# Two-layer grouped-query attention: transposing the probabilities of four batch steps per session, with Q projections in row tiles between them

## The chip, the core and the metric

The kernel runs on one NeuronCore of a Trainium2 chip. The metric is the device time of one execution in microseconds, as the median of a few runs. TensorE is called PE here (PEld for its weight loads), VectorE DVE, ScalarE ACT, GpSimd POOL, and SP is the queue that issues every DMA.

## The reference

Two independent problems, A and B, of the same shape; their results stand side by side in the output.

```python
B, Sq, D = 16, 80, 576
Hq, Hkv, Sk, Dh = 32, 16, 512, 128           # bf16 inputs
q = (x @ wq).reshape(B, Sq, Hq, Dh).transpose(0, 2, 1, 3)
k = jnp.repeat(k_cache, 2, axis=1)           # k_cache, v_cache: (B, Hkv, Sk, Dh)
v = jnp.repeat(v_cache, 2, axis=1)
p = softmax(einsum("bhqd,bhkd->bhqk", q, k) * Dh ** -0.5)
o = einsum("bhqk,bhkd->bhqd", p, v)
out = o.transpose(0, 2, 1, 3).reshape(B, Sq, Hq * Dh) @ wo
# concatenate([out_A, out_B], axis=-1)
```

## The kernel before

**Units.** One batch of one "octet" (four K/V heads, so eight query heads of 80 rows each) is a unit, called a batch step here; there are 128 of them, U = 0 to 127. The 640 query rows of a unit are cut into five blocks of 128: four "mains" (k = 1 to 4, one K/V head each) and one "remainder" (k = 0, 32 rows of each of the four heads).

**What PE does.** For every eight batches and one octet, eight Q projection steps (each two heads by four batches) are computed from `xT` and `wq_sb`: D = 576 is contracted as four full chunks of 128 rows (L565) and a tail of 64 rows, for which the two heads stand in the two halves of the array's rows (L578, `tile_position=(64 * h, 0)`). Scores of a main are one full matmul of 512 columns (L692); those of a remainder are four matmuls of 32 output columns side by side (L679, `tile_position=(0, 32 * g4)`). After the softmax the probabilities P are transposed on PE (L749) in halves of 64 rows, two at a time, against a 64-wide identity. Attention times V is L797, the output projection L843. So PE works in three shapes of the array: full (L565, L692, L797, L843), row tiles (L578, L749) and column tiles (L679). The text calls a stretch in one shape a visit, and a change from one shape to the next a switch.

**What the others do.** DVE takes each block's row maximum out of PSUM (L701), ACT the exponential with its sum (L705), DVE the reciprocal (L711), POOL the normalisation (L714). Copies out of PSUM (Q: L590/L591, transposed P: L766/L767 and, for remainders, L775/L776, attention output: L811, output projection: L855, L872) are shared between DVE and ACT. PSUM has eight banks of 512 fp32 columns.

**A transposition session.** Two units are transposed together: 80 matmuls into five banks, the remainders of both in the fifth. P lives in 12 slots for mains and 4 for remainders (`NPA`, `NPR`), its transpose in two (`NPT`). Scores of two units are made as a group (`GR = 2`), both remainders first. The attention output `oT` is kept for all sixteen batches of an octet pair; the output projection goes over five row blocks for one half of the 576 columns and then for the other (`n % NRT, n // NRT`).

**The order.** Nothing is scheduled at run time. Each operation belongs to a stream (for example `T`: transposes, `PV`, `S`: scores, `K`: loads of K), and the string `ORDER` lists one letter per operation: it fixes the order on every engine, the PSUM bank of each result (digits), and by an apostrophe whether ACT instead of DVE makes a copy. `finalize` then adds the semaphores. A load is also tied to the PE operation that stands ahead of it in the table, so it is not issued earlier than that:

```python
if op.eng == "pe":
    last_pe = op
elif op.paced and last_pe is not None:      # names that begin with "ld"
    deps[id(last_pe)] = last_pe
```

K comes in loads of 1 MB for two units (a transposing DMA, L645, in three slots), V in loads of 0.5 MB for one (L649, six slots).

Of the kernel before, what the change touches and what calls it, by code (L numbers as in the profile page):

```python
# [12 lines left out]
GR = 2  # L13
# [3 lines left out]
NPA = 12  # L17
NPR = 4
NPT = 2
NS = 32  # L20
# [26 lines left out]
NSS = 6  # L47
# [19 lines left out]
wDCCCCC'B'Httcc7cj6j4d3Ad5wBtgl7102wKNGtl6'F'E'H'Gk45Fj7mj1xNwj0b6utwwtbj3j2c7acxwNt'yw'Atc1cj4c6mj0cd7wBANwCC
DCCCDCCj3c1cttud6BCtgl2451'HwKNG'Fl0DCCj6t'Ej7b2j3bwwNGw'Ftt'ytj5c1j6cc0ms7QwNwttd4j2cj5d3CCc6ANwYwc'BtCCDCc1'
ActCQgl7026'K'H'Gl5Fk34'B'F'EGk07xaj1wuxtNxxuuj6mb5c3bj2uwyNwcd4d0mj7gwt'Atj6c5wNHtt'Kcj3b1j4j7wBbc6j2tNwwtCCC
DCCDCCyj3ctCwl0415'Atl7mwFN'Gj6c2tcj0wd4d3g'F'Gtmaj5wNBEwNj2'Htamj7c6j1cc4d0cwtAwNwKtDCCCCCDCCc6d5cc2ct'BACgl6  # L70
374tBK'H'Gl1Fk25Fmj0'E'Gxb3j4mc7cj6j1bwuxwNt'Autj2c7cc0wtwyNCj4j5cj3d6twNwwtwBNtDCDCCCCCCb1j4twAbc5acd0tt'y'Bg
l4327'K'Hl5G'Fk60'Ek14m'FGxxc2j7b3uxuNwNDCCCCj6ubctwxAc1j0c'ytuw'Bc5cj2d6c7j3tNwAwCCDcj4d1d5ttwNBad0tCggCl3274
'K'HNHG'F'Kl1mE'F'Gk56Uj2j3b0c4mj7cbCDCxwtc1cj2wtuwxABwj3'yutwj4j0d1b5j6Nwtttc2NwwCDCtcaj3j7bmtNAwwCCCCd0c2cmd
6'yt'Btd5Umggl7432K'H'Hl0j6GEwNNb1CCCCj3j4w'K'F'GtwFtc5cbj2c7aj0j6ct'A'ywwNwBtc4d1j3cd5j2td7c0cRwNwBt'AttDCDCC
Cd4ggl6203H'H'KKl1F'Gk54'Ek67'F'Gxxuc0cc1cj3b2j5uxxwBwNNuutt'ACCc4j6Rcmc1bwAj3j7cj4b5j0wBNw'yttwNwCDCCCDCCd1j3
bad6tttwt'yd2d7ggl5340'K'KHHNl6'G'Fk27j1'G'FExxj3uc4cc5j6j0cuANwwwc2mmcj4m'Bc7tcUaUb5t'Btd1j7wNwAtd3wDCCCCCj6t
wtj2mbd4wNtd0tNyDCCCggl2567'HKKN'Hl3'G'FCCCk14'F'GEj0j5xuxj6c2cc3j7cwAwwu'Btttb1j2bc4cj3d6mamj0wwNAttwNwtj4d7D
CCCCCDwd5c2ctd3tggyBHN'Kl4201l6'Gj7KHEw'Fj5j2j3ac0'F'Gcc4cwwNBwtt'Ac6j1cd7j4c0cb5t'At'BwNj2d3j6bCDCCCtwwNwtd0C
CDCCt'ytd2ggl5641H'K'HKl3F'Gk02'Ek76x'Guxc5mj1cb4c0Nwu'At'Fcj2bj1c5CCDxBNwywutmcj4maj3mc0b2cNwwxB'Attutj5d1j7b
j4d6Qd0wwwNCCCCDCCttNytd3ggl4725K'HKl1Fk36Ej4'G'F'H'Gj7xxNCCCDCj2c0mucc1cj5c3Awwu'Btwtwcb0j6bj4tNwAwtd2aQj7c3c  # L80
j1d5mCCtwNwtCDCtd6td4gNByNHgl1037'K'HKFl2'Gk56'Ej4'G'Fxj0CCCuxwwc1cc7j2cj3'Atutc5mcb1wwAaj4j6bc0j5tBwNwtttwyNj
2mcd7d4DCCDCCwNBtd1Cd3tggl6520'Hl7NKF'K'G'H'Gj3Cwj4b6j0tEwwbj2j1c3d5c'Fttwj7c4j0ct'ywNAwNCCCCDt'BtQc3cj1d2wwaQ
c4d6mmgcd7CCCDtt'AKHBgl0351'H'Kl4F'G'F'Ek62Gk70xb4c3j1cc5xuuxxwcj2j6bBwN'Autuj7j3mc5cc1j0ctzwwNwwNCDCCDCCCt'A'
Btb4j5tNwbd7j2ad3td6twzNtd1ggl0425'H'HCCCCKNKl7k16Exx'F'GOj3j0c2'G'FcuwAwumOj5c4j7cc1c'Bc2tcmb6j4wt'BtwANwj3d0
aj1d2j5mbtwtNwwtCCCCDCDNztd7Cd4tggl5163'K'Hl2'FNKHGk47'ECCDCj1'Gxj0j5'Fj6xc3ucwc2uOcc4Xctb7j1wAwAw'BtttwNbj3c0
j2cj4d5wtwzwNttmaOd1d7td2CCCDCCBggl4603'Hl5'H'KKNE'G'FCd7j2j1wwc0cc6cj4'F'GBwN'Attc3cc6cj5mj0j2b1Nwwwt'A'Bttj6
d3CCCDCCDwNtCCj5abd0twtd2zggmOl4156'K'KHHl7'Gk32k10'FxxE'Guu'FNxNxb4bc3cj6c2wzCCCDCucj7w'Auj1c5OXcj3c0mw'Btt'A
j2cmb6j7mwBNwttj0mabj3d4CtwNwzwd1tCCDtCgl7652Ht'Kl0k41'Gj6xNwb3'F'E'Gtj5d2Fwutd7j6c0cj4bc5xNwut'AwzNj1cd3d0XOj
6wwCCCCDCCtt'Bj4gmg'K'Htj1c5cOwNHwCDc7d2ttcad6j4NKA'BgCCCUl1035wKNG'Hl7k62Et'G'F'Fj4b0q3j7j1abc5xwx$wu'#tutNDC
DCCCcc3j4d6cwwAzBttc7cj5j1d0wwNtCCtROmc3cd4d2BANggl5371K'H'K'FHl6Gj4j2d5'FEwGwc6cj3mj7b0'AtwwNtc1cj4CCDCCtc2wc  # L90
amUtc6j3cANwt'Bj7CDj2bd4wNwzCCd1ttt'BCd3ggl2076'KH'KHl4G'Fk51G'Ek23'Fxmc6cOc0cj7j4xub5xNwwu'B'Attuj0bj7c1j6acw
xzNwu'AtwNtOc4mcj2Xb5j3j0d1CCCCDCwBwtttd7j4d6bNwwNztCCCDDCCtd3ggl4520HKNF'Kl1'H'Gk37Gj5'E'Fxj4XRmUc6Xcc1d2cuj0
c3xwwAut'Bcd7j6wtc5j1gj4ctwNAwwCDCj0b3t'KtBNwHttUj6d7mbmad4j5NwzCCCCtgl3120wNGF'K'Hl6tk47DCCCCj1d5'F'Ex'Gj6Oxu
wj2c3cc0acd4uwA'Btwc7j0d3ctNwAd1tgtgNHc6j2'KHw'KDCCCcj7'Bd3wCtl0645tGl1j2d7j6FwwN'F'E'Gj0twgc4cd5c1j2tt'ANKwcc
6cj0c7q4mmOcNBHwt'Aj3j1$w'#t'BtwNb6d2j7btwCCDCCCCDCtCgl1340'KzHl6'FOk27Fk15ax'G'E'Gxuxuj3mb6c4cbj7j2c0NxwAwuut
# [12 lines left out]
2cj0j5c7cb3uu'AwwNxbj2tb1j0tu'BCCyNwwttj3j5mmj6c4cj2d7wwNwwNtt'ADCCCCCDCbc0cd3Ud4Ut'y'Btd6ggl2051KKHNN'Hl3a'GC
CCCDk64E'Fj0xj7c5'F'Gxucc2j3j1cuAwj6b5ww'Btttwc2j4d0mcd7tRj3wNwNwAbj1tDCCCCtc6cd2w'ytd5tggBNKl4631'H'KNHl7'Fk2
0'Ej5GxxDC'G'Fuj4mac3cmj6c1j7cuwwAb2c0cj3'BtwtwtANwj5d1ttwCbc0j4cj7d3wNwyttBd6td5aCCCCDCgCgml2047'KNHKl3'Gj5HE  # L110
w'Fj1'G'Fj0j6c4cwNAc7tcaOc3cc5j2t'BANwwwcj4mb7'BtttDCCCCCwNtj5d1d0CCCDwd3mj2btwytd6ggl5427H'K'KHl1G'Fk06'Ek45G
x'Fxc7cc1cu'Auc2cmc3cj0BNxwCj1'A'ButxwNb6bj3wuttj7j0b4j1j2bawwyNtj6d7twwNtCCCDCCDtd0wyNd5CCCtd1ggl2643H'K'Hl0'
Gk57KENxx'FCCCDj6j1mQ'G'Fuc4j2cj3c0cuAww'Btwb5c4j0ctj6twANwwttmmabj7d1c4j2cd3mtCDwNwBNytd0CCCd6tggl2547'H'HKKN
l1'G'Fk60ECCj5'F'Gxj3Qc4cj2c1cj7xuwwAuab6j0c4ttj5bcc3wwNBwwtt'Attj2j1d7cd4d5NwwNBytCDCCCDCd0tCgg'KHl1326'Kl4'F
j0j7GHww'E'Fttb3j4bj2c1j0wGNwwNt'yCCCDCCCj5ad6cc4j3cmtwwN'Attc7j2cd0wBAttd5c1cd4CDCBggl1372HK'K'Hl6G'Fk54k10'E
'F'Gxc7cc6j3j2cxuAuj7mj5wNNxxwb4t'Bmbj6b3mmwywututtj2bwwzNc0cOj7Qaj4c1md5cttwNAwCDCCCCDCCd6d3d2CgttBHNgl0147'K
'Hl6NKG'Fk25CCCCD'Ej1xj3'F'Gwuc0Qcc6j4cj7xwBtb2j1j6mautwwAttbj5c3cwNwNwttj0d4c7cmd1d6CCDCtd5gwABztgl3072'KCl1N
HKGH'Fk54'Ej3'G'FxNwj0c7cOj6c2cj1uAwttc5cb7j0wxNwwAbt'Buttj6j3c2d5j1acd0wwwNttd4CCDCDCCCCCd6tggBzN'K'H'Kl2713C
Cl0HGF'Ej4d6j5'G'Fc1cc7cj3wNwAwttc0j4cj2'B'AtNwwj5c7d1Ocmmd0tCDCCj4t'BNwwtb3j2mtbwDCCCtd4azggl2357O'K'HKl1G'Fk
64Ek32'F'G'Hxc5cj7c0cc1u'A'Bcxxwxuuutc6cj0mb5BANj6j1j3bwwNzwtDCCj4b0ambj5ttNwtNwwtd7j2d3twztmd6d4CCCCCDCggl105  # L120
2'HKNH'Kl3'GCOk67j0'F'F'Gj4ExxNwwuutb1c5cj6c3cj2j7btwwAwNt'Btj4mc0cc5j3j6cd2wCDCttd7AwwNtCDCCCCd4td0zNBggl6513
# [16 lines left out]

class _Op:
    __slots__ = ("eng", "key", "seq", "emit", "reads", "writes", "dsem", "stream", "alloc", "alt",  # L140
                 "deps", "signals", "sidx", "waits", "clock", "name", "hard", "parts", "paced")


class _Sched:
# [33 lines left out]
    def arrange(self):  # L178
# [778 lines left out]
```

## Time and profile before

| | before |
|---|---|
| median of 3 runs (lowest, highest) | 713.65 us (713.46, 714.14) |
| span of the profiled execution | 711.6 us, 26075 instructions, granted clock 1.000 |
| profiled execution's own time | the runs' 713.46 to 714.14: 1.9 to 2.5 us lie around the span |
| PE busy | 702.5 us (99%) |
| ACT, DVE, POOL busy | 645.5, 613.3, 431.9 us |
| DMA | 160.72 MB, mean 226 GB/s |

Busy times count an instruction from its start to its end. Instructions of PE overlap each other, so how long a group of matmuls holds PE is read from the start of the group to the start of the next one, not from its busy time.

### The profile page before, as it was taken

How to read it: one execution, taken by the hardware profiler on the slowest of the kernel's cores; microseconds unless marked ns; L12 is line 12 of the kernel's file. 1: busy time of each engine (PE TensorE's matmuls, PEld its weight loads, DVE VectorE, ACT ScalarE, POOL GpSimd, SP SyncE). 2: the span in 40 equal slices, each digit the busy share in tenths (PEclk: the TensorE clock that was granted, in tenths of full speed). 3: DMA queues.
4: the chain of work that ended last, by engine and by line, in shares of the span. 5: the costliest groups of instructions: out<-in, count | busy, mean ns of one | idle time of the engine just before them, and what ended most of it. 6: DMA issues, size and time to landing. Idle time of an engine off the chain costs nothing.

```text
span 711.6 us, 26075 instructions
## 1 busy us (share of the span) xinstructions
PE 702.5 (99%) x10820; PEld 512.5 (72%) x10820; DVE 613.3 (86%) x1339; ACT 645.5 (91%) x1772; POOL 431.9 (61%) x650
## 2 busy tenths in 40 slices
PE   8999999999999999999999999999999999999998
PEld 4567677777777777777767777777777777777767
DVE  2999898889798888899989888889888989889894
ACT  2999999999999999989999899999999989999893
POOL 0567666656565566656656576565756666477572
DMA  8999999989899998999989999999799989888762
GB/s 210 252 256 260 261 245 239 253 230 255 182 250 230 246 223 217 222 254 253 227 233 242 226 261 177 270 214 218 215 237 242 241 214 253 220 210 188 171 157 82
DMA packets 374166, 160.72 MB, mean 226 GB/s; under 512 B 278560, under 2 KB 370976, under 8 KB 374048
## 3 DMA queue, kind: packets, MB, share of 16 engines
q1 hardware_dynamic: 374048, 159.05, 96.4%
q8 instruction: 86, 1.41, 0.8%
q14 instruction: 32, 0.26, 0.1%
HBM read 87.65 MB, written 2.95 MB: 127 GB/s over the span
## 4 chain that ended last, share of the span: by engine, by line
PE 96%; ACT 1%; DMA 1%; DVE 1%; issue 0%; SPq 0%
PE ps L843 22%; PE ps L797 20%; PE ps L565 19%; PE ps L692 16%; PE ps L749 11%; PE ps L679 4%; PE ps L578 4%; DMA wq_sb<-in_A_wq_dram 1%; ACT p_sb L705 1%; DVE negmax L701 1%; ACT pT L766 0%; ACT oT L811 0%; PE ps L421 0%; SPq L400 0%; DVE qT L591 0%
## 5 line engine op out<-in xcount | busy, mean ns | idle before, releaser
L714 POOL TENSOR_SCALAR p_sb<-p_sb,rinv 128x512 bf16<-128x512 bf16 x640 | 430.1, 692 | 261.2 <-DVE rinv L711 260.8
L705 ACT ACTIVATE p_sb<-ps,negmax 128x512 bf16<-128x512 f32 x640 | 439.3, 717 | 15.8 <-DVE negmax L701 13.3
L701 DVE TENSOR_REDUCE negmax<-ps 128x1 f32<-128x512 f32 x640 | 409.8, 677 | 17.5 <-PE ps L692 9.5
L797 PE MATMUL ps<-pT,v_sb 128*128 128x160 bf16 x2048 | 186.0, 233 | 0.9 <-ACT p_sb L705 0.5
L797 PEld LDWEIGHTS ps<-pT,v_sb 128*128 128x128 bf16 x2048 | 154.9, 98 | 38.8 <-ACT pT L775 3.0
L843 PE MATMUL ps<-wo_sb,oT 128*128 128x288 bf16 x1280 | 180.9, 286 | 0.7 <-issue 0.7
L692 PE MATMUL ps<-kT,qT 128*128 128x512 bf16 x512 | 170.4, 380 | 1.2 <-issue 0.9
L565 PE MATMUL ps<-xT,wq_sb 128*128 128x320 bf16 x1024 | 165.1, 299 | 1.6 <-DMA wq_sb<-in_A_wq_dram 1.2
L843 PEld LDWEIGHTS ps<-wo_sb,oT 128*128 128x128 bf16 x1280 | 123.2, 98 | 45.7 <-DVE pT L767 1.8
L705 ACT ACTIVATION_READ_ACCUMULATOR p_sb<-ps,negmax 128x1 f32 x640 | 149.2, 233 | 0.0
L565 PEld LDWEIGHTS ps<-xT,wq_sb 128*128 128x128 bf16 x1024 | 97.1, 98 | 43.9 <-issue 1.7
L766 ACT COPY pT<-ps 128x512 f32<-128x512 f32 x181 | 100.5, 606 | 6.7 <-PE ps L749 4.8
L591 DVE TENSOR_SCALAR qT<-ps 128x320 bf16<-128x320 f32 x119 | 54.6, 483 | 39.8 <-PE ps L578 39.6
L749 PEld LDWEIGHTS ps<-ident,p_sb 64*128 64x128 bf16 x5120 | 82.6, 95 | 7.8 <-ACT oT L811 1.1
L749 PE MATMUL ps<-ident,p_sb 64*128 64x64 bf16 x5120 | 85.8, 190 | 0.5 <-DVE qT L591 0.4
L590 ACT ACTIVATE qT<-ps 128x320 bf16<-128x320 f32 x137 | 55.3, 446 | 21.8 <-PE ps L578 21.4
L811 DVE CAST oT<-ps 128x320 bf16<-128x320 f32 x143 | 67.6, 478 | 5.4 <-PE ps L797 4.9
L692 PEld LDWEIGHTS ps<-kT,qT 128*128 128x128 bf16 x512 | 45.6, 97 | 27.2 <-ACT pT L766 6.6
L767 DVE COPY pT<-ps 128x1024 bf16<-128x1024 bf16 x75 | 50.0, 685 | 9.8 <-PE ps L749 9.5
L811 ACT CAST oT<-ps 128x320 bf16<-128x320 f32 x113 | 49.3, 450 | 3.9 <-PE ps L797 3.8
L711 DVE RECIPROCAL rinv<-rowsum 128x3 f32<-128x3 f32 (+1 forms) x256 | 39.8, 159 | 3.6 <-ACT p_sb L705 3.3
L679 PE MATMUL ps<-kT,qT 128*32 128x512 bf16 x512 | 36.8, 383 | 0.0
(33 smaller groups left out, 149.8 us busy)
## 6 DMA issues: line engine op xcount, KB each, us to landing
v_sb<-in_A_v_cache_dram SPq DMA_DIRECT2D x64, 512.0 KB, 5.4
v_sb<-in_B_v_cache_dram SPq DMA_DIRECT2D x64, 512.0 KB, 4.9
wo_sb<-in_A_wo_dram SPq DMA_DIRECT2D x8, 576.0 KB, 5.8
wo_sb<-in_B_wo_dram SPq DMA_DIRECT2D x8, 576.0 KB, 5.9
wq_sb<-in_B_wq_dram SPq DMA_DIRECT2D x4, 1024.0 KB, 6.0
out_dram<-osb SPq DMA_DIRECT2D x40, 72.0 KB, 3.8
wq_sb<-in_A_wq_dram SPq DMA_DIRECT2D x8, 256.0 KB, 4.6
wq_sb<-in_A_wq_dram SPq DMA_DIRECT2D x2, 1024.0 KB, 6.0
```

What stands on the lines that cost most here:

```text
L565: last = e.matmul(ps[:, vbq[h].phys, QO:QO + 320], lhsT=wq_sb[:, wsl, ck, hi * 128:(hi + 1) * 128], rhs=xT[:, half, ck, n0:n0 + 320], star ...
L590: return e.activation(dst, src, AF.Identity, scale=SCALE)
L679: last = e.matmul(ps[32 * g4:32 * g4 + 32, vb_.phys, :], lhsT=qT[:, qsl_, bl_, g4 * 160 + 128:g4 * 160 + 160], rhs=k_of(U_, g4), start=Tru ...
L692: return e.matmul(ps[:, vb.phys, :], lhsT=qT[:, qsl, bl, gl * 160:gl * 160 + 128], rhs=k_of(U, gl), start=True, stop=True)
L701: return e.tensor_reduce(negmax[:, si:si + 1], ps[:, vb.phys, :], axis=AX.X, op=AluOpType.max, negate=True)
L705: return e.activation(p_sb[:, psl, :], ps[:, vb.phys, :], AF.Exp, bias=negmax[:, si:si + 1], scale=1.0, accum_out=rowsum[:, ss, k:k + 1])
L714: return e.tensor_scalar(p_sb[:, psl, :], p_sb[:, psl, :], rinv[:, ss, k:k + 1], 1.0, op0=AluOpType.mult, op1=AluOpType.mult)
L749: last = e.matmul(dst, lhsT=p_sb[64 * h:64 * h + 64, psl2[i_][k_], j * 128:(j + 1) * 128], rhs=ident[64 * h:64 * h + 64, 64 * h:64 * h + 6 ...
L766: return e.copy(dst.bitcast(F32), ps[:, vb.phys, :].rearrange("p (j n) -> p j n", j=4))
L797: last = e.matmul(ps[:, vo.phys, off:off + 160], lhsT=v_sb[:, vs, gl, j * 128:(j + 1) * 128], rhs=pT[:, pts, j, :, 32 * gl:32 * gl + 32], ...
L811: return (e.copy if en == "act" else e.tensor_copy)(dst, src)
L843: last = e.matmul(ps[:, vb.phys, 0:DC], lhsT=oT[:, sp_ * (HH // 2) + i, rb * 128:(rb + 1) * 128], rhs=wo_sb[:, 2 * c3 + sp_, i, :], start= ...
```

## The change

One session now transposes four units (two at the start and at the end of the program): first the remainders of all four into two banks, then each unit's mains into two banks of their own, ten banks in all, given out as they come free. Q projection steps may be made in "tiled" form: each of the four 128-row chunks as two 64-row matmuls for the two heads at once, in which the two halves of the array change heads half-way, so that the whole step is in row tiles like the transposes. The table marks 52 of the 128 steps so, and puts them between the transposes. The code for scores in tiled form is there too, and the table never asks for it. Scores of four units form a group (`GR = 4`). The attention output is kept for eight batches, and the output projection goes over both column halves of a row block in turn. P has 20 and 5 slots, its transpose four. The table `ORDER` is another one throughout.

```diff
-GR = 2
+GR = 4
+TG = (2, 2, 2, 2) + (4,) * 29 + (2, 2)
-NPA = 12
-NPR = 4
-NPT = 2
-NS = 32
+NPA = 20
+NPR = 5
+NPT = 4
+NS = 40
-NSS = 6
+NSS = 9
 ORDER = """
-XVSXSVvv!Pn0o7To3ZSSao1'ZPZe0e6r4o3TWo2We7e5!YZhIhf1'Z'J'IJr0e4e2e6e7e5hhTe3'I'Y'I'JJe4Te7hahf0X'I'I'Jj6j2k5f4
...
+c1cc3cCRDb6bBb2bBRR
@@ arrange
             if op.alt:
                 op.eng = op.alt[other]
+            elif other:
+                for a, v in op.tiled.items():
+                    setattr(op, a, v)
@@ buffers
-        oT = sb("oT", [128, HH, NPP * NROW], BF16)
+        oT = sb("oT", [128, HH, NROW], BF16)
@@ Q projection
+                def em_qh(e, ph, cks, ends, hp=hp, wsl=wsl, half=half, n0=n0, vbq=vbq):
+                    last = None
+                    for ck in cks:
+                        for h in range(2):
+                            r = slice(64 * (h ^ ph), 64 * (h ^ ph) + 64)
+                            hi = 2 * hp + h
+                            last = e.matmul(ps[:, vbq[h].phys, QO:QO + 320], lhsT=wq_sb[r, wsl, ck, hi * 128:(hi + 1) * 128],
+                                            rhs=xT[r, half, ck, n0:n0 + 320], start=(ph == ck == 0), stop=(ph == 1 and ck == 3),
+                                            tile_position=(64 * (h ^ ph), 0))
+                    for h in range(2) if ends else ():
+                        r = slice(64 * h, 64 * h + 64)
+                        last = e.matmul(ps[:, vbq[h].phys, QO:QO + 320], lhsT=wt[r, wsl, hp, :], rhs=xT[r, half, 4, n0:n0 + 320],
+                                        start=False, stop=False, tile_position=(64 * h, 0))
+                    return last
...
+                    tiled = dict(emit=lambda e, f=em_qh, h=h: f(e, h, range(2) if h else range(4), not h),
...
@@ transposes
-            if U % 2:
-                (pa, ua, ta), (pb, ub, tb) = pend
...
+            if len(pend) == tgs[0]:
+                done, pend = pend, []
+                n_ = tgs.pop(0)
+                vrt = [S.bank() for _ in range(2)]
+                def em_trr(e, done=tuple(done), vrt=vrt):
...
+                for i_, (psl_, u_, t_) in enumerate(done):
+                    vtp = [S.bank() for _ in range(2)]
...
@@ output projection
-                        r, c3 = divmod(n, NOC) if prob == 1 and hh == NPAIR - 1 and half == NPP - 1 else (n % NRT, n // NRT)
+                        r, c3 = divmod(n, NOC)
```

How the two tables place the work on PE, at the session that transposes units 28 and 29 before and the one that transposes units 24 to 27 now. Rows are runs of equal instructions in program order. Before, the way into the session (the last row is the first of its 80 transposes, which go on in the same way, remainder and main in turn):

```order
L692 MATMUL ps<-kT,qT 128x512
L797 MATMUL ps<-pT,v_sb 128x160 x8
L843 MATMUL ps<-wo_sb,oT 128x288 x8
L565 MATMUL ps<-xT,wq_sb 128x320 x4
L692 MATMUL ps<-kT,qT 128x512
L565 MATMUL ps<-xT,wq_sb 128x320 x4
L692 MATMUL ps<-kT,qT 128x512 x2
L843 MATMUL ps<-wo_sb,oT 128x288 x8
L565 MATMUL ps<-xT,wq_sb 128x320 x8
L578 MATMUL ps<-xT,wt 128x320 x4
L749 MATMUL ps<-ident,p_sb 128x64
```

Now, the whole session, from the tail of an ordinary Q step (L608) to the last transposes; L574 and L579 are Q steps in tiled form with their tails, L783 and L811 the transposes of remainders and mains:

```order
L608 MATMUL ps<-xT,wt 128x320 x2
L574 MATMUL ps<-xT,wq_sb 128x320 x8
L579 MATMUL ps<-xT,wt 128x320 x2
L608 MATMUL ps<-xT,wt 128x320 x2
L783 MATMUL ps<-ident,p_sb 128x64 x32
L574 MATMUL ps<-xT,wq_sb 128x320 x8
L811 MATMUL ps<-ident,p_sb 128x2x32 x32
L574 MATMUL ps<-xT,wq_sb 128x320 x8
L579 MATMUL ps<-xT,wt 128x320 x2
L811 MATMUL ps<-ident,p_sb 128x2x32 x64
L574 MATMUL ps<-xT,wq_sb 128x320 x8
L811 MATMUL ps<-ident,p_sb 128x2x32 x32
```

What moved: four Q chunks at a time stood in full form among scores and output projections, and 80 transposes followed on the tails; now the chunks of two Q steps stand in row tiles among 160 transposes, with no score and no output projection in between. Over the whole program PE's order has 227 switches before (88 into row tiles, 50 into column tiles, 89 into the full array) and 170 now (62, 43, 65).

The queue SP from the load of K for units 30 and 31 on. Before (L645 loads K, L649 V, L538 a piece of wq):

```order
L645 DMA_TRANSPOSE kT<-in_A_k_cache_dram 128x4x1024
L649 DMA v_sb<-in_A_v_cache_dram 128x4x512 x3
L538 DMA wt<-in_A_wq_dram 64x4x128
L645 DMA_TRANSPOSE kT<-in_A_k_cache_dram 128x4x1024
L538 DMA wt<-in_A_wq_dram 64x4x128
L649 DMA v_sb<-in_A_v_cache_dram 128x4x512 x2
L645 DMA_TRANSPOSE kT<-in_A_k_cache_dram 128x4x1024
L649 DMA v_sb<-in_A_v_cache_dram 128x4x512
L645 DMA_TRANSPOSE kT<-in_A_k_cache_dram 128x4x1024
```

Now (L676 loads K, L680 V):

```order
L676 DMA_TRANSPOSE kT<-in_A_k_cache_dram 128x4x1024 x2
L680 DMA v_sb<-in_A_v_cache_dram 128x4x512 x6
L676 DMA_TRANSPOSE kT<-in_A_k_cache_dram 128x4x1024
L680 DMA v_sb<-in_A_v_cache_dram 128x4x512
L676 DMA_TRANSPOSE kT<-in_A_k_cache_dram 128x4x1024
L680 DMA v_sb<-in_A_v_cache_dram 128x4x512 x4
L676 DMA_TRANSPOSE kT<-in_A_k_cache_dram 128x4x1024 x2
```

What moved: loads of K came one by one between loads of V, and now come in places two at a time, since a group of four units reads two loads of K at its start.

More of the change, by code (lines that the diff above doesn't have):

```diff
@@ L67 @@
[L67 to L71, printed above, removed]
@@ L140 @@
     __slots__ = ("eng", "key", "seq", "emit", "reads", "writes", "dsem", "stream", "alloc", "alt",
-                 "deps", "signals", "sidx", "waits", "clock", "name", "hard", "parts", "paced")
+                 "deps", "signals", "sidx", "waits", "clock", "name", "hard", "parts", "paced", "tiled")
 class _Sched:
@@ L152, in bank, with add @@
         return _VB(self.nvb)
-    def add(self, eng, key, emit, reads=(), writes=(), dsem=None, name="", stream=None, alloc=(), alt=None, hard=(), parts=()):
+    def add(self, eng, key, emit, reads=(), writes=(), dsem=None, name="", stream=None, alloc=(), alt=None, hard=(), parts=(), tiled=None):
         op = _Op()
@@ L168, in add @@
         op.parts = list(parts)
+        op.tiled = tiled
         op.paced = name.startswith("ld")
@@ L568, in em_qp @@
                         return last
-                    S.add("pe", x + 0.001 * h, em_qp, reads=[R(("wq", wsl, hp), wv)] + xr,
-                          writes=[R(vbq[h], 0)] + [R(("qT", qsl, bl, 2 * hp + h), goct) for bl in range(b0, b0 + 4)],
-                          name="qp%d.%d.%d" % (goct, m, h), stream="Q" if goct > 1 else "Q%d" % goct, alloc=[vbq[h]])
+                    tiled = dict(emit=lambda e, f=em_qh, h=h: f(e, h, range(2) if h else range(4), not h),
+                                 reads=wqr + xr + ([] if h else wtr + xtr), writes=vbw + ([] if h else qtw[0] + qtw[1]),
+                                 alloc=[] if h else list(vbq), hard=list(qops))
+                    qops.append(S.add("pe", x + 0.001 * h, em_qp, reads=wqr + xr, writes=[vbw[h]] + qtw[h],
+                                      name="qp%d.%d.%d" % (goct, m, h), stream="Q" if goct > 1 else "Q%d" % goct, alloc=[vbq[h]],
+                                      tiled=tiled))
                 def em_qt(e, hp=hp, wsl=wsl, half=half, n0=n0, vbq=vbq):
@@ L580, in em_qt @@
                     return last
-                S.add("pe", x + 0.01, em_qt, reads=[R(("wt", wsl, r), wv) for r in range(2)] + xtr,
-                      writes=[R(v_, 0) for v_ in vbq], name="qt%d.%d" % (goct, m), stream="QT" if goct > 1 else "QT%d" % goct)
+                S.add("pe", x + 0.01, em_qt, reads=wtr + xtr, writes=vbw, name="qt%d.%d" % (goct, m),
+                      stream="QT" if goct > 1 else "QT%d" % goct,
+                      tiled=dict(emit=lambda e, f=em_qh: f(e, 1, range(2, 4), False), reads=wqr + xr))
                 for h in range(2):
@@ L627, in bass_concat_heads__gqa_block_cached__gqa_block_cached__near_ridge_kernel @@
         pend = []
-        group = []
+        tgs = list(TG)
         for U in range(NSU):
@@ L659, in bass_concat_heads__gqa_block_cached__gqa_block_cached__near_ridge_kernel @@
             psls = []
+            vbs = [S.bank() for _ in range(5)]
+            qks = []
             for k in range(5):
@@ L669, in bass_concat_heads__gqa_block_cached__gqa_block_cached__near_ridge_kernel, with em_qkr @@
                 psls.append(psl)
[L670 removed]
+                vb = vbs[k]
                 if k == 0:
[L673 to L689 removed]
+                    def em_qkr(e, vb=vb, U=U, qsl=qsl, bl=bl):
+                        last = None
+                        for g4 in range(4):
+                            last = e.matmul(ps[32 * g4:32 * g4 + 32, vb.phys, :],
+                                            lhsT=qT[:, qsl, bl, g4 * 160 + 128:g4 * 160 + 160], rhs=k_of(U, g4),
+                                            start=True, stop=True, tile_position=(0, 32 * g4))
+                        return last
+                    S.add("pe", tq, em_qkr, reads=[R(("qT", qsl, bl, i), goct) for i in (1, 3, 5, 7)] + [R(("kT", ks), U)],
+                          writes=[R(vb, 0)], name="qkr%d" % U, stream="SR", alloc=[vb])
                 else:
@@ L806, in bass_concat_heads__gqa_block_cached__gqa_block_cached__near_ridge_kernel, with em_oev @@
                         hb = 8 * (q % 2) + 4 * pr
[L808 removed]
+                        def em_oev(e, en, vo=vo, hb=hb, row=bl * SQ):
                             dst = oT[:, hb:hb + 4, row:row + SQ]
```

259 lines of the change are left out of this document (134 added, 125 removed).

## The prediction, made before the changed kernel ran

> **What bounds the kernel now.** I read the page first, then the chain of work that ended last, then PE's own waits, and then PE in order of time around one session. The page, its busy shares and the chain's shares by engine:
>
> ```profile
> span 711.6 us, 26075 instructions
> PE 702.5 (99%) x10820; PEld 512.5 (72%) x10820; DVE 613.3 (86%) x1339; ACT 645.5 (91%) x1772; POOL 431.9 (61%) x650
> PE 96%; ACT 1%; DMA 1%; DVE 1%; issue 0%; SPq 0%
> ```
>
> The list of waits for PE alone (who it waited for, total, times, longest; these are its longest):
>
> ```profile
> PE ps L373 <- DVE wo_sb L366: 1.2, 1, 1.2
> PE ps L565 <- DMA wq_sb<-in_A_wq_dram: 1.2, 1, 1.2
> PE ps L692 <- issue: 0.9, 2, 0.5
> PE ps L843 <- issue: 0.7, 1, 0.7
> PE ps L797 <- ACT p_sb L705: 0.5, 1, 0.5
> ```
>
> PE is never seen waiting for anything but a few short times: it is the bound, and the time is what its instructions hold it for. A busy PE can still lose time where one matmul starts later than the one before it requires, which the busy rows do not show. So I took prices from starts. Three pieces of the chain, each of equal matmuls in full form that follow each other:
>
> ```profile
> 152.10 1.63 PE ps L565 x12
> 470.43 1.38 PE ps L797 x20
> 472.95 1.96 PE ps L843 x16
> 578.19 0.43 PE ps L692 x2
> ```
>
> One Q chunk (320 columns) holds PE 1.63/12 = 0.136 us, attention times V 1.38/20 = 0.069, an output projection matmul 1.96/16 = 0.1225, a main's scores 0.43/2 = 0.215. Now one session in order of time (start, length, then the instruction):
>
> ```profile
> 281.93 0.38 PE L692 MATMUL ps<-kT,qT 128*128 128x512 bf16 x1
> 282.14 1.25 PE L565 MATMUL ps<-xT,wq_sb 128*128 128x320 bf16 x8
> 283.33 0.31 PE L578 MATMUL ps<-xT,wt 64*128 64x320 bf16 x2
> 283.48 1.34 PE L749 MATMUL ps<-ident,p_sb 64*128 64x64 bf16 x80
> 284.74 0.62 PE L679 MATMUL ps<-kT,qT 128*32 128x512 bf16 x8
> 285.29 0.39 PE L692 MATMUL ps<-kT,qT 128*128 128x512 bf16 x1
> 285.51 1.14 PE L843 MATMUL ps<-wo_sb,oT 128*128 128x288 bf16 x8
> ```
>
> The eight Q chunks hold PE from 282.14 to 283.33, 1.19 us, where 8 x 0.136 = 1.09: **0.10 us is lost where the array goes from full form to row tiles.** The eight column-tile matmuls run four at a time, so two groups of 0.215 = 0.43, and they hold PE 0.55: 0.12 is lost on the way back to full form. Out of row tiles the price is seen at the start of the program:
>
> ```profile
> 9.94 0.45 PE L578 MATMUL ps<-xT,wt 64*128 64x320 bf16 x4
> 10.31 0.72 PE L565 MATMUL ps<-xT,wq_sb 128*128 128x320 bf16 x4
> ```
>
> Two pairs of tails are 2 x 0.136 = 0.27, and 0.37 pass: 0.10. With that, the 80 transposes (40 pairs, 1.26 us) are 40 x 0.029. The whole is then 1280 x 0.1225 + 2048 x 0.069 + 1024 x 0.136 + 512 x 0.215 + 128 groups of four L679 x 0.215 + 2560 pairs of L749 x 0.029 + 128 pairs of L578 x 0.136 = 667 us, and 227 switches (counted in PE's order) at 0.10 to 0.12 are another 23.6. The remaining 21 us are the start, the end and the few waits.
>
> **The time it is set against.** The span is 711.6; the three runs have a median of 713.65, so 2.05 us lie around the span, and I take that as unchanged. The terms below are added to 713.65.
>
> **Fewer switches.** The order has 170 instead of 227. PE leaves the full form 65 times instead of 89, row tiles 62 instead of 88, column tiles 43 instead of 50: 24 x 0.10 + 26 x 0.10 + 7 x 0.12 = 5.8 us less. All of it lies on the path, since PE is 96% of the chain. What could be late next in a place where a switch goes is a copy out of PSUM or a load; both have terms below.
>
> **Q in row tiles.** 52 of 128 Q steps are tiled: 416 full chunks become 832 matmuls of 64 rows, 416 pairs. A pair must hold PE at least the 0.136 that 320 columns take in either form, so a gain is excluded. The other end is the single pair of tails in the session above: from 283.33 to 283.48, 0.15. If every pair cost that, 416 x 0.014 = +5.8 us. The nearest row is the piece with two pairs in a run (9.94 to 10.31), which leaves 0.136 for each, so the extra belongs to the first of a visit; I take one of 0.014 for each of some 25 long sessions, +0.4, and keep 0 to +5.8.
>
> The weight loads might stand open, for there are twice as many. Where two pairs of tails follow each other, PEld and PE show:
>
> ```profile
> 305.25 0.11 PEld L578 LDWEIGHTS ps<-xT,wt 64*128 64x128 bf16 x4 [0.26 <-issue]
> 305.25 0.45 PE L578 MATMUL ps<-xT,wt 64*128 64x320 bf16 x4
> 305.54 1.34 PE L749 MATMUL ps<-ident,p_sb 64*128 64x64 bf16 x80
> ```
>
> and the group of these loads in the list by line (count, busy, mean ns):
>
> ```profile
> L578 PEld LDWEIGHTS ps<-xT,wt 64*128 64x128 bf16 x256 | 8.4, 94 | 20.6 <-issue 20.2
> ```
>
> All four loads are done 0.11 us after the first began, while the first pair still runs, and the four matmuls take 0.29 us, so the second pair's loads cost nothing. [...]
>
> **Copies out of PSUM.** Rows of the groups by line (count, busy, mean ns):
>
> ```profile
> L766 ACT COPY pT<-ps 128x512 f32<-128x512 f32 x181 | 100.5, 606 | 6.7 <-PE ps L749 4.8
> L767 DVE COPY pT<-ps 128x1024 bf16<-128x1024 bf16 x75 | 50.0, 685 | 9.8 <-PE ps L749 9.5
> L811 DVE CAST oT<-ps 128x320 bf16<-128x320 f32 x143 | 67.6, 478 | 5.4 <-PE ps L797 4.9
> L811 ACT CAST oT<-ps 128x320 bf16<-128x320 f32 x113 | 49.3, 450 | 3.9 <-PE ps L797 3.8
> L591 DVE TENSOR_SCALAR qT<-ps 128x320 bf16<-128x320 f32 x119 | 54.6, 483 | 39.8 <-PE ps L578 39.6
> L590 ACT ACTIVATE qT<-ps 128x320 bf16<-128x320 f32 x137 | 55.3, 446 | 21.8 <-PE ps L578 21.4
> ```
>
> By the order, DVE's copies of transposed P go from 101 to 129 and six of half size (+28 x 0.685 + 6 x 0.35, half of a whole one, = +21), its copies of attention output from 143 to 128 (-7); ACT's go from 219 to 185 and six halves (-34 x 0.606 + 6 x 0.3 = -19) and from 113 to 128 (+7). So DVE gets some 14 us more and ACT 12 less, out of idle times of 98 and 66. PE's matmuls cover them, and I cost them at nothing. The cover is thinnest inside a session. The one shown in the order is 20 pairs of Q or tails and 80 pairs of transposes, 20 x 0.136 + 80 x 0.029 = 5.0 us. In it fall ten copies of P and up to eight of Q: with half on each engine, ACT has 5 x 0.606 + 4 x 0.446 = 4.8 us and DVE 5 x 0.685 + 4 x 0.483 = 5.4. No scores come meanwhile, and exponentials left over from before go on, for which P now has slots for five units. If the cover is gone, DVE is 0.4 us late per session.
>
> **Loads.** No bytes are added, and SP issues the same DMAs in another order. A group of four units reads two loads of K at its start, so one of them is needed sooner. I counted PE's work, at the prices above, from the PE operation that a K load stands behind in the table to its first reader: before, 7 of 64 loads have less than 11.5 us, now 22, most of them 10.2 to 11.4. The trace has for loads of K, from issue to landing:
>
> ```profile
> L645 SPq DMA_TRANSPOSE kT<-in_A_k_cache_dram x32: 3988/5704/9672, 6.9 to 322.2; - x32
> DMA to landing us min/median/max: 6.1/8.9/12.1
> ```
>
> The median leaves 2 us, the longest does not reach. I take two loads late by 0.3, +0.6; the ends are 0 and 22 x (12.1 - 10.8) = +29. Loads of V and wo have between 7 and 30 us by the same count, and I add nothing for them. Those queued behind a K load on SP wait for its issue (5.7 us in the median) as they do now.
>
> **Start.** Before, a first Q step was computed between the transposes of x; now it stands behind all of them, and the first K load stands one quarter of a weight load earlier in SP's queue. I put +0.2, between -0.5 and +1: the waits of 1.2 us in PE's list are all that either order could win or lose there.
>
> **Sum.** -5.8 + 0.4 + 0.6 + 0.2 = -4.6, so 713.65 - 4.6 = 709.0 us.
>
> **The rivals.**
>
> *Loads of K come late (slower).* Place: the first scores of a group of four. Where SP issues two loads of K back to back, the second begins 5.7 us after the first. For it: the 12.1 in the row above and the 22 short distances. Against it: PE's waits name no K load, with seven such distances already. If half of the 22 land after 12.1 us, that is 11 x 1.3 = 14 us: 709.0 - 0.6 + 14 = 722.4. It decides from 5.2/22 = 0.24 us late per load, where the other terms' gain is gone.
>
> *Copies bind inside the sessions (slower).* DVE's 5.4 us against 5.0 make PE wait 0.4 in each of 29 long sessions, +11.6: 720.6. Against it: a copy may slip behind the session, where PE has other banks, and instructions of one engine overlap a little at their ends.
>
> *Tiled pairs are dearer (about the same).* At 0.15 per pair the time is 709.0 - 0.4 + 5.8 = 714.4. A bank that goes from one row half to the other, once in each of the 52 tiled steps, may cost as much as a switch: 52 x 0.10 = 5.2, so 713.8. [...]
>
> *Weight loads stand open (slower).* At a mean of about 0.09 us a load, 416 x 0.09 = +37: 746. The four loads in 0.11 us speak against it.
>
> *More is won.* PE's waits after the start (the last three rows of its list, 2.1 us) go too: 707.
>
> That the switches do not go is excluded by the order.
>
> **How the numbers follow.** Forecast 0.66 (707.5 to 711.5) and more won 0.06: together 0.72 for faster. Tiled pairs dearer 0.09: the same. K late 0.10, copies 0.07, weight loads 0.02: 0.19 for slower. About 0.2% (1.4 us) is what a measurement of this kernel can tell from no change, so faster means under 712.2 and slower over 715.1. The range takes in the forecast, more won and dearer tiles and the lower edge of the slower cases: 705.5 to 716.
>
> **What would show it.** Right: the pieces of L574 at 0.136 per pair, L574 and L811 following each other with no loss, PE still at 96% of the chain, and 57 fewer gaps of 0.10. Wrong: PE waiting for kT at L709 or L718, or for DVE pT inside a session; or a pair of L574 above 0.14, which would take the gain without any wait in the list.

## The result: 744.62 us, slower by 4.4%, and the profile after

| | before | after |
|---|---|---|
| median of 4 runs (lowest, highest) | 713.56 us (711.82, 714.14) | 744.62 us (739.97, 749.65) |
| ratio, 95% interval | | 1.0441, 1.0392 to 1.0491 |
| profiled execution: device time, span, granted clock | 711.6 (span), 1.000 | 749.65, 747.8, 0.984 |

709.0 us was forecast, with a range of 705.5 to 716.0. Ratios, here and below, are to the kernel before as it was measured again beside each run, so they are not always the quotient of two medians shown. The page of after, the rows that answer to those shown of before (busy shares, then DMA queues with packets, MB and share, then the chain by engine):

```profile
span 747.8 us, 26926 instructions
PE 710.9 (95%) x11236; PEld 520.8 (70%) x11236; DVE 624.7 (84%) x1351; ACT 641.2 (86%) x1766; POOL 431.4 (58%) x650
...
q8 instruction: 89, 1.46, 0.8%
...
PE 91%; issue 4%; ACT 3%; DMA 1%; DVE 0%
```

q8 is the DMA queue that the page calls "instruction"; its packets are of 16 KB. Its row before:

```profile
q8 instruction: 86, 1.41, 0.8%
```

PE was 99% busy and is now 95%, and the chain has 4% of "issue", time in which PE waited for nothing that the profile shows. PE's own waits after (who for, total, times, longest):

```profile
PE ps L811 <- issue: 21.2, 12, 3.7
PE ps L783 <- issue: 2.5, 2, 2.2
PE ps L574 <- issue: 2.4, 2, 1.9
PE ps L718 <- ACT p_sb L745: 2.1, 1, 2.1
PE ps L891 <- issue: 1.8, 2, 0.9
...
PE ps L709 <- DMA kT<-in_A_k_cache_dram: 0.3, 1, 0.3
```

PE stands in the middle of its sessions, among the transposes (L811, L783) and the tiled Q (L574), up to 3.7 us at a time, and for no other engine. One such place, PE alone in order of time:

```profile
303.78 0.71 PE L574 MATMUL ps<-xT,wq_sb 64*128 64x320 bf16 x8
304.32 0.25 PE L811 MATMUL ps<-ident,p_sb 64*128 64x64 bf16 x5
307.31 0.58 PE L811 MATMUL ps<-ident,p_sb 64*128 64x64 bf16 x27 [2.75 <-issue]
307.82 1.39 PE L709 MATMUL ps<-kT,qT 128*32 128x512 bf16 x16
```

After five transposes of a run of 32 nothing starts for 2.7 us, and then the other 27 follow. The same stretch by windows of 2 us (busy time by engine, then PE's granted clock, DMA share, GB/s):

```profile
302.00:304.00 2.00, 2.00 (x102) 1.79 (x95) 1.68 (x4) 1.92 (x5) 2.00 (x4) 1.00 1.05 358
304.00:306.00 2.00, 0.57 (x13) 0.33 (x9) 0.68 (x1) 0.96 (x2) 0.96 (x2) 1.00 1.07 360
306.00:308.00 2.00, 0.69 (x31) 0.58 (x35) 0.00 (x0) 0.07 (x1) 0.00 (x0) 1.00 0.32 90
308.00:310.00 2.00, 2.00 (x21) 0.80 (x14) 1.73 (x3) 2.00 (x5) 0.00 (x0) 0.60 0.07 16
310.00:312.00 2.00, 2.00 (x14) 1.53 (x12) 1.31 (x4) 2.00 (x7) 1.67 (x3) 0.55 0.46 68
```

Two things are to be seen. In the first row PE takes 102 matmuls and 95 weight loads in 2 us; in full form, at 0.069 each, the shortest price measured there, it would take 29. And behind the stall the granted clock is 0.60 and 0.55 in these rows (0.50 from 308.4 to 311.8), so the stall is followed by a second loss: in another such stretch 16 matmuls of L891 held PE 3.14 us, where 16 take 1.96 at full clock:

```profile
237.84 3.14 PE ps L891 x16
262.11 1.96 PE ps L891 x16
```

**Where PE stops.** In the trace I numbered PE's records (weight loads, matmuls, semaphore instructions; 22818 in all) in order of time. Six of the eight longest gaps of after, and all in the full swing of the kernel before, each from one start to the next, with the number of records ahead of the gap, that number's remainder by 256, and the q8 packet of 16 KB last begun:

```
after   gap ends  long   records  rem.   q8 packet          before  gap ends  long   records  rem.   q8 packet
        163.98    2.36    4801    193    161.62-162.69              181.43    0.48    5313    193    178.95-179.88
        258.54    2.87    7617    193    255.89-257.00              187.88    0.56    5569    193    185.62-186.51
        307.31    2.93    9153    193    305.02-305.97              246.56    0.60    7361    193    243.95-245.08
        334.85    3.90    9921    193    332.48-333.44              344.86    0.63   10433    193    342.34-343.47
        403.41    2.62   11969    193    400.96-401.98              448.58    0.76   13761    193    446.00-447.02
        429.90    2.52   12737    193    427.59-428.57              682.60    1.02   21185    193    679.60-680.79
```

Every stall stands at the same remainder. It holds beyond this table: in the traces of all seventeen runs, those below included, leaving out the first 100 and the last 12 us, two starts of PE lie over 0.7 us apart in 230 places, and 227 of them have remainder 193. The page counts 89 packets on q8, one for 22818/89 = 256.4 records, and the kernel before had 86 for 21971. My reading of these counts, which the experiments test: PE's instructions come in blocks of 256, a packet of q8 each, and PE stops where a block is used up and the next has not come. At the 22 stalls of after, the packet of the next block begins 0.7 to 3.9 us (median 2.6) after PE has passed the boundary before, lands 1.1 us after it began (median), and PE goes on 1.3 to 1.6 us after that. From a boundary passed to PE going on, these stalls show 3.6 to 6.5 us. Behind the first three blocks, 256 records last 5.0 to 11.8 us in the kernel before; in the changed kernel, taken from its run with light loads (below), 2.8 to 14.3, and 28 of 85 blocks less than 5.5. At every stall the packet began only after the boundary before, 0.7 us behind it at the earliest, so PE had less than one block of 256 left when it began.

The 22 stalls at remainder 193, each less the usual distance of two starts there, sum to 35.4 us in after's profiled execution, against 3.5 in six before.

### The profile page after: what moved, and what is told of

It reads as the page before. It is cut to its first block, busy times and chain, and to the rows that moved or that the text cites. A ratio compares the mean times of both kernels' runs of the same rounds, so it can differ in the third digit from the quotient of the medians.

```text
span 747.8 us, 26926 instructions
## 1 busy us (share of the span) xinstructions
PE 710.9 (95%) x11236; PEld 520.8 (70%) x11236; DVE 624.7 (84%) x1351; ACT 641.2 (86%) x1766; POOL 431.4 (58%) x650
## 4 chain that ended last, share of the span: by engine, by line
PE 91%; issue 4%; ACT 3%; DMA 1%; DVE 0%
PE ps L891 21%; PE ps L844 19%; PE ps L718 14%; PE ps L592 10%; PE ps L811 8%; PE ps L574 8%; PE ps L709 4%; ACT p_sb L745 2%; PE ps L783 2%; PE ps L608 2%; PE ps L579 1%; DMA wo_sb<-in_A_wo_dram 1%; DMA wq_sb<-in_A_wq_dram 1%; PE ps L381 0%; DVE negmax L741 0%
## 5 line engine op out<-in xcount | busy, mean ns | idle before, releaser
L745 ACT ACTIVATE p_sb<-ps,negmax 128x512 bf16<-128x512 f32 x640 | 437.9, 710 | 26.7 <-DVE negmax L741 25.2
L844 PE MATMUL ps<-pT,v_sb 128*128 128x160 bf16 x2048 | 180.1, 235 | 1.5 <-issue 0.9
L891 PE MATMUL ps<-wo_sb,oT 128*128 128x288 bf16 x1280 | 179.7, 288 | 1.9 <-issue 1.8
L844 PEld LDWEIGHTS ps<-pT,v_sb 128*128 128x128 bf16 x2048 | 154.6, 99 | 36.2 <-issue 5.6
L718 PE MATMUL ps<-kT,qT 128*128 128x512 bf16 x512 | 159.6, 383 | 2.1 <-ACT p_sb L745 2.1
L891 PEld LDWEIGHTS ps<-wo_sb,oT 128*128 128x128 bf16 x1280 | 124.9, 99 | 46.6 <-issue 3.6
L745 ACT ACTIVATION_READ_ACCUMULATOR p_sb<-ps,negmax 128x1 f32 x640 | 145.2, 227 | 0.0
L823 ACT COPY pT<-ps 128x512 f32<-128x512 f32 x152 | 86.4, 600 | 38.8 <-PE ps L811 37.7
L811 PE MATMUL ps<-ident,p_sb 64*128 64x64 bf16 x4096 | 79.4, 191 | 21.2 <-issue 21.2
L592 PE MATMUL ps<-xT,wq_sb 128*128 128x320 bf16 x608 | 96.2, 299 | 0.4 <-DMA wq_sb<-in_A_wq_dram 0.3
L811 PEld LDWEIGHTS ps<-ident,p_sb 64*128 64x128 bf16 x4096 | 73.0, 95 | 30.6 <-issue 21.9
L824 DVE COPY pT<-ps 128x1024 bf16<-128x1024 bf16 x104 | 69.4, 685 | 25.3 <-PE ps L811 24.7
L592 PEld LDWEIGHTS ps<-xT,wq_sb 128*128 128x128 bf16 x608 | 57.8, 98 | 29.0 <-issue 1.1
L574 PE MATMUL ps<-xT,wq_sb 64*128 64x320 bf16 x832 | 73.9, 297 | 2.4 <-issue 2.4
L718 PEld LDWEIGHTS ps<-kT,qT 128*128 128x128 bf16 x512 | 47.1, 98 | 28.7 <-ACT p_sb L745 4.5
L858 DVE CAST oT<-ps 128x320 bf16<-128x320 f32 x128 | 60.8, 482 | 5.2 <-PE ps L844 4.8
L574 PEld LDWEIGHTS ps<-xT,wq_sb 64*128 64x128 bf16 x832 | 36.1, 94 | 11.9 <-issue 2.3
```

The lines of the kernel that those rows point to most:

```text
L574: last = e.matmul(ps[:, vbq[h].phys, QO:QO + 320], lhsT=wq_sb[r, wsl, ck, hi * 128:(hi + 1) * 128], rhs=xT[r, half, ck, n0:n0 + 320], star ...
L592: last = e.matmul(ps[:, vbq[h].phys, QO:QO + 320], lhsT=wq_sb[:, wsl, ck, hi * 128:(hi + 1) * 128], rhs=xT[:, half, ck, n0:n0 + 320], star ...
L718: return e.matmul(ps[:, vb.phys, :], lhsT=qT[:, qsl, bl, gl * 160:gl * 160 + 128], rhs=k_of(U, gl), start=True, stop=True)
L745: return e.activation(p_sb[:, psl, :], ps[:, vb.phys, :], AF.Exp, bias=negmax[:, si:si + 1], scale=1.0, accum_out=rowsum[:, ss, k:k + 1])
L811: last = e.matmul(dst[:, :, 32 * (k_ - 1):32 * k_], lhsT=p_sb[64 * h:64 * h + 64, psl_[k_], j * 128:(j + 1) * 128], rhs=ident[64 * h:64 * ...
L823: return e.copy(dst.bitcast(F32), ps[:, vb.phys, :].rearrange("p (j n) -> p j n", j=4))
```

## The experiments

Theory "supply": PE stops where it has used up a block of 256 instructions before the next has come. A stretch is called dense where small matmuls follow each other so closely that this can happen. Rivals: "tiles" (the Q steps in row tiles, or their banks, hold PE) and "copies" (copies out of PSUM come late, and the profile names the wait wrongly). "Stalls" below are always the gaps at remainder 193 in the profiled execution, summed in the same way.

**The boundary moved.** Semaphore increments that nobody waits for were put among PE's matmuls between the sessions, one instruction each, so that the boundaries fall elsewhere. A table says how many stand ahead of which matmul. One of the matmuls, and the function without the lines that read the table:

```diff
-                            last = e.matmul(ps[:, vo.phys, off:off + 160],
+                            last = pad(e).matmul(ps[:, vo.phys, off:off + 160],
...
+def pad(e):
...
+    for _ in range(_Pad.at.get(_Pad.n, 0)):
+        e.sem_inc(pad.sem, 1)
+    _Pad.n += 1
+    return e
```

> The changed kernel with some 1550 one-line semaphore increments put among PE's full-form matmuls, so that the boundary of a block of 256 instructions always lies about 45 instructions ahead of a long session. Theory 'supply' (PE gets its instructions in blocks of 256, the next block is asked for at a boundary and arrives 3.2 to 6.5 us later, and a long session uses 256 instructions in 2.8 to 3.6 us): the stalls in the sessions fall from 35 us to between 5 and 15, the time to 718 to 730. Rival 'tiles' (the Q steps in row tiles, or the change of their banks between the halves, hold PE) and rival 'copies' (copies out of PSUM come late): nothing that they speak of is changed, 740 to 750, or more by what the increments cost (0.051 us each, if nothing hid them).

> The same with about as many increments (some 1620), put so that the boundary lies 220 instructions ahead of each long session. 'Supply': a session now has a whole block inside it every time, the stalls rise from 35 to between 43 and 57 us, 755 to 770. 'Tiles' and 'copies': the same time as with the boundary at 45, since the work and its order are the same.

Measured: 762.53 us (ratio 1.0679, 1.0632 to 1.0725) and 795.44 (1.1167, 1.1127 to 1.1207). Both times are missed. The first had come out otherwise than said: the boundaries lay some 0 to 30 instructions ahead of most sessions, not 45; in the second they lay 161 to 210 ahead. The stalls of the first are 42.8 us, those of the second 56.0, as expected for it. The two do the same work and differ by 33 us, but only 13 of these are stalls: the increments were not free and stand at other places, and set beside each other instruction by instruction they account for some 15, the stretches at half clock for 5. So the times alone do not decide between the theories, and the first was made again:

> The changed kernel with semaphore increments again, now with the positions counted in the built program (in the first try the boundary had come to lie 0 to 30 instructions ahead of the sessions instead of 45), 38 instructions ahead of every long session, and only among matmuls of 122 ns and more that are well away from a session. 'Supply': with 5 us from asking to going on, the block times leave 9 us of stalls (5 at 4.5 us, 22 at 5.5 us): 716 to 732. Otherwise 756 to 764 as in the first try.

Measured: 770.21 (1.0801, 1.0778 to 1.0824); the time is missed, by the increments: two between matmuls took 0.302 us, three 0.452. What was asked of it is in PE's waits:

```profile
PE ps L891 <- issue: 5.2, 13, 1.7
PE ps L811 <- issue: 3.4, 3, 2.1
...
PE ps L574 <- issue: 0.2, 1, 0.2
PE ps L783 <- issue: 0.2, 1, 0.2
```

In the sessions (L811, L783, L574) 26.1 us of issue have become 3.8, with the same tiles, banks and copies; some 18 us of stalls stay in the whole run, most of them outside the sessions. In the second run, with the boundary far ahead, the same rows are 29.7 for L811 and 19.8 for L574:

```profile
PE ps L811 <- issue: 29.7, 17, 3.1
PE ps L574 <- issue: 19.8, 9, 4.0
```

**The loads taken away.**

```diff
+                if U >= 16:
+                    return e.dma_start(few[:, ks, :], kc_ap[b, 4 * q, 0:128, 0:16])
```

and the same for V, in the kernel after and in the kernel before (there with `0:8`). Both go on computing with the old K and V.

> The changed kernel in which the loads of K and V from the 17th unit on bring 4 KB instead of 1 MB and 0.5 MB, into a tile of their own (the arithmetic goes on with the old K and V). 'Supply': if the block of instructions waits behind the loads' packets, it comes within 2 to 3 us, the stalls go, 709 to 716; if its way takes 5 us by itself, 740 to 750. 'Tiles' and 'copies': 740 to 750.

> The kernel before with the loads of K and V from the 17th unit on cut to 2 KB, as in the run of the changed kernel with light loads (708.57). 'Supply': PE of the kernel before loses only 3.5 us to late blocks, so it gains little, 708.5 to 713, and what stands between it and 708.57 is the change's own gain without stalls, 0 to 4.6. If the loads held PE in some other way (through SBUF, or by K and V landing late), it falls as far as the changed kernel did, by 36 us, to 677.

Measured: 708.57 (0.9939, 0.9924 to 0.9954) and 709.53 (0.9947, 0.9932 to 0.9962). The page of the changed kernel without the loads, and PE's longest wait in it (L816 is L811):

```profile
span 707.0 us, 26926 instructions
PE 697.7 (99%) x11236; PEld 515.5 (73%) x11236; DVE 622.9 (88%) x1351; ACT 639.9 (91%) x1766; POOL 433.1 (61%) x650
...
PE 96%; ACT 2%; issue 1%; DVE 0%
```

```profile
PE ps L816 <- issue: 4.6, 5, 2.3
```

The changed kernel gains 36 us when its loads go, the kernel before 4. At the 22 boundaries ahead of after's stalls, the q8 packets now begin 0.7 us after the boundary in the median, 2.4 at the most, where the median was 2.6; over all boundaries the medians are 0.7 and 1.8. The stalls are 5.9 us, and none in the kernel before. So the packets begin later beside the loads, by 1.9 us in the median at these boundaries, and without that delay the long sessions lose 5.9 us to stalls instead of 35.4.

> The changed kernel with only the loads of K cut to 4 KB; V is loaded as before. 'Supply', if a block of instructions waits mostly behind the transposing loads of K: 709 to 718. If it waits behind bytes of any kind: half of the 36 us stay, 722 to 732.

> The changed kernel with only the loads of V cut; K is loaded as before. If blocks wait behind the transposing loads of K: 735 to 745. If behind bytes of any kind: 722 to 732.

Measured: 718.90 (1.0084, 1.0064 to 1.0103) and 718.39 (1.0074, 1.0046 to 1.0103), stalls 15.1 and 12.2; at the same 22 boundaries the packets begin 1.0 us after them in the median in both. Neither case expected came: beside either kind of load alone the packets begin later than with light loads (1.0 against 0.7 us) and 12 to 15 us of stalls stay, and each taken away gives back more than half of the 36 us.

**A dense visit with no other part of the change.** In the kernel before:

```diff
-                    for pair in list(zip(rems + mains, mains + rems))[n0_:n1_]:
+                    for pair in 2 * list(zip(rems + mains, mains + rems))[n0_:n1_]:
```

> The kernel before, with every transpose of P made twice into the same place: sessions of 160 instead of 80 transposes, no Q in row tiles, no other bank, no further copy. 2560 more pairs at 0.029 us are 74 us: 788. 'Supply': sessions of over 320 instructions in 2.3 us stall as well, another 60 to 107 us, 848 to 895. 'Tiles' and 'copies': 788.

Measured: 923.70 (1.2977, 1.2928 to 1.3027), stalls 103.7 us, the longest 6.1. The page's clock row (tenths, 40 slices) and PE's first wait:

```profile
PEclk9999989998999999999998989999999998999999
```

```profile
PE ps L749 <- issue: 62.2, 25, 5.9
```

So neither tiled Q nor ten banks are needed for it. What lies above the expected 895 fits the clock, a term that I had left out: 0.964 granted over 911.8 us is up to 33 us, and set instruction by instruction beside its run with light loads (the last of the next three), 63 of the 85 us between them are stalls and 27 lie in the stretches at half clock. The same with fewer repeats, and with light loads:

> The kernel before with a quarter of every session's transposes made a second time: 100 instead of 80, so 208 dense instructions with the tails. The 640 pairs more are 18.6 us: 732. 'Supply' with 4.5 to 5.5 us from asking to going on and the block times of the kernel before: 6 to 25 us of stalls, 738 to 757. If a dense visit cost in proportion to its length (the 210 us of twice the transposes, divided by four): 766.

> The same with half of the transposes made again: 120, so 248 dense instructions. 1280 pairs are 37 us: 751. 'Supply': 28 to 55 us of stalls, and some us more where the clock is lowered behind long ones: 779 to 815. In proportion: 818.

> The kernel before with every transpose made twice and the loads of K and V from the 17th unit on cut to 2 KB. 709.5 + 74 = 784 without stalls. 'Supply' with two parts of the wait, the loads' (gone) and the way's own (0.8 + 1.1 + 1.4 = 3.2 us): 34 us of stalls stay, 810 to 825, where 924 were measured with the loads. If the loads were all of it: 784.

Measured: 751.59 (1.0511, 1.0452 to 1.0571), 787.17 (1.1025, 1.0969 to 1.1081), 827.50 (1.1612, 1.1569 to 1.1655). Visits of 168 (the kernel before), 208, 248 and 328 dense instructions have stalls of 3.5, 22.1, 34.6 and 103.7 us: from 168 to 208 they grow sixfold. Without the loads 41.5 us stay with the longest visits, so there stalls stay even without them, as the expectation had it from its estimate of 3.2 us for the block's own way; the time is 2.5 above the range given.

**Tiled Q undone at its places**, so that sessions are cut up. In `ORDER`, each of the 52 tiled steps loses its apostrophes (`d` and `g` are the parts of a Q step, the digits its two banks):

```diff
-'d62
-'d
-'g
+d6
+d2
+g
```

> The changed kernel with all 52 tiled Q steps in full form at the places where they stand, so that every long session is cut into visits of row tiles of 2 to 100 matmuls. By the order there are 373 switches of shape instead of 170, 203 x 0.105 = 21 us more. 'Supply': no block's 256 instructions fall into one dense stretch any more, the 35 us of stalls go: 745 - 35 + 21 = 731, and less by what the lowered clock after the stalls cost: 720 to 732. 'Tiles': the same. 'Copies' (ten banks of transposed P in one session, and Q between them): the stalls stay and the switches come on top, 755 to 766.

Measured: 745.94 (1.0461, 1.0445 to 1.0476). The range was missed: 19.3 us of stalls stay, since a block still lasts as little as 3.4 us where pieces of a session are half a microsecond of Q apart. Against the changed kernel's 744.62 this is no difference: what tiled Q saves in switches (21 us by the expectation's count) it loses in stalls (16) and clock (0.984 against 0.995, up to 8).

**K in halves, increments one at a place, and both.** For the halves, `ORDER` has 56 more letters for loads of K:

```diff
-            kw = 2 if goct >= ILV and U // 2 >= KSP else 1
+            kw = 2 if U < 16 else 1
```

> The changed kernel in which each load of K from the 17th unit on comes as two loads of one unit (0.5 MB), the first of them some 3 us of PE's work earlier in the order, the second where the whole load stood. 'Supply' with blocks of instructions waiting behind the load in progress: they wait less, about 4.2 instead of 5.0 us from asking to going on, the stalls fall from 35 to about 20 us, 725 to 738. If the wait does not depend on the size of a load: 740 to 750.

> The changed kernel with semaphore increments as in the run with the boundary 41 instructions ahead, but at most one between two matmuls and spread evenly over the full-form work between sessions, where the traces show one to be free (0.069 to 0.069, 0.122 to 0.123 us between matmuls) and two or more at 0.151 each. 'Supply': the 30 us that the increments cost go, the stalls stay at 10 to 18: 713 to 724. If the increments cost as much in this way, or if the stalls come back: over 735.

> Both together: K in halves, and one increment at a place so that a boundary lies 40 instructions ahead of every long session. 'Supply' with 4.2 us from asking to going on leaves 3 to 8 us of stalls by the block times: 704 to 714. If halves change nothing: as the run with spaced increments alone.

Measured: 751.65 (1.0514, 1.0450 to 1.0578), 758.42 (1.0628, 1.0596 to 1.0660), 743.39 (1.0454, 1.0405 to 1.0504). All three were missed. Halves alone leave the stalls at 33.3 us and the median begin over all boundaries at 1.8, as it was: with loads of K of 0.5 MB instead of 1 MB the packets came no sooner here. With spaced increments the stalls were 37.5, though the boundaries lay 36 to 42 instructions ahead of nearly every long session: in the stalls it now took 4.5 to 9.9 us from boundary to PE going on, more than the 5 that I had reckoned with, and blocks that last about 5 us gave no margin. PE's waits there:

```profile
PE ps L811 <- issue: 14.1, 10, 3.4
...
PE ps L783 <- issue: 2.4, 2, 1.4
PE ps L574 <- issue: 2.2, 1, 2.2
```

So with the boundary in nearly the same place, 18.7 us of issue stay in the sessions where the second try with increments had 3.8. The blocks into the 27 long sessions last as long in both, 5.4 us in the median without the stall; but their packets begin 3.2 us after the boundary with spaced increments, and 2.1 in the second try. So the place of the boundary counts (49.5 us of issue stood there with it far ahead), and the delay of the packet counts beside it. Nor were spaced increments free: instruction by instruction against the run with light loads they add some 13 us, most of it between matmuls of L844. Both changes together leave 18.7 us of stalls. What decides when a packet begins, up to 6.9 us after the boundary, is not settled beyond the medians with and without loads (1.8 and 0.7 us in the changed kernel). No version here beats the kernel before with its loads; 709.53, its time with light loads and without stalls, is 0.5% less.

## Why the prediction was wrong, point by point

- **Fewer switches, -5.8; tiles +0.4; start +0.2: right as a sum;** no run tells the three apart. With light loads the spans are 707.5 before and 707.0 after, the latter with 5.9 us of stalls: 707.0 - 5.9 - 707.5 = -6.4, where -5.2 had been reckoned for these three. The chain of after shows four pairs of tiled Q at 0.135 each and 16 pairs of transposes at 0.029, following each other with no loss:

```profile
118.34 0.54 PE ps L574 x8
118.88 0.47 PE ps L811 x32
119.35 0.98 PE ps L709 x16
```

- **Rivals "tiled pairs dearer" and "weight loads open":** did not happen: over the 91 runs of eight tiled Q matmuls in after's trace the median is 0.136 us a pair.
- **Copies at nothing: right.** PE's waits name no copy in a session. The row `L718 <- ACT p_sb L745: 2.1` ends at record 7105, remainder 193: a stall by supply that the list gives to ACT.
- **Loads of K, +0.6: right as put,** two loads late by 0.3 (PE waited 0.3 us for one). But loads cost the kernel in another way: with light loads it took 708.57 us, and the packets of q8 began 0.7 instead of 1.8 us after the boundary.
- **The step that failed** is the bound itself: "the time is what its instructions hold it for". The sum has no term for the stops at remainder 193, 3.5 us before and 35.4 after. The first sign stood in the rows that I quoted, `L692 <- issue: 0.9` and `L843 <- issue: 0.7`, two small waits for nothing; I called them a few short waits, and under "more is won" even let them go. Their remainders would have told. The change took 80 to 84 matmuls per visit to 196 to 200, and the shortest time of a block from 5.0 us to 2.8.
- **The sum with the missing terms:** 711.6 - 3.5 (stalls before) - 6.4 + 35.4 (stalls after) + 11.4 (matmuls that start later after one another than usual, outside the stalls; set beside the run with light loads, nearly all of it lies in seven stretches of 3.4 us at half clock) = 748.5, measured 747.8. The rivals and the signs of being wrong named late K, late copies, dearer pairs and open weight loads; none of them made the time, and none was about how PE gets its instructions.

## What to carry to other kernels

Count PE's instructions, not only its microseconds: in these runs PE stopped where 256 of them (a matmul is two: the page has 11236 of PE and 11236 of PEld) were used up before the next packet had landed. From the boundary before to PE going on it took 3.6 to 6.5 us in the changed kernel's stalls and up to 9.9 with spaced increments. Joining dense visits of small matmuls saved a switch of 0.10 us and cost stalls of up to 3.9 us, with 3.4 us at half clock behind seven of them; with visits of 168 instructions the program lost 3.5 us to stalls, with visits of 208 it lost 22. "Issue" in PE's waits is to be looked up, by the number of instructions ahead of it, even where it is small.

## What the runs showed of the hardware that I had not expected

- The packets of 16 KB on q8 (86 before, 89 after) stand in the page among those of the core's 16 DMA engines, 0.8% of their span, and they begin later beside loads: over all blocks the median is 0.6 and 0.7 us after the boundary without the loads (kernel before, kernel after), 2.3 and 1.8 with them.
- One standalone semaphore increment between two matmuls on PE left the median distance of their starts as it was (0.069 and 0.069 us for L844, 0.122 and 0.123 for L891), but with spaced increments 119 of 567 between matmuls of L844 cost over 0.03 us, 9.8 us in all. Where two or more stood together, each took 0.151 us (L891: two 0.302, four 0.603).
- At seven of the nine stalls of over 2.2 us in after, PE's granted clock was 0.50 for 3.4 us (from 308.4 to 311.8, for one), beginning between 0.1 us before the stall's end and 1.4 us after it; at the other two (2.87 us at 258.54, 2.22 at 568.47) it stayed at 1.00.
